# Moving units, scalings, a cast and two loads by a unit or two in a fused attention and GEGLU kernel

## The chip, the cores and the metric

The kernel runs on one core of a Trainium2 chip. The metric is device time in microseconds (us) of one execution. In the profiles' lines PE is TensorE (PEld its weight loads), DVE is VectorE, ACT is ScalarE, POOL is GpSimd and SPq is SyncE, which issues transfers. Profiles time the span, some 2.1 us shorter than the time of the run.

## The reference

```python
# q, k, v: (8, 8, 576, 64) f32; w_gate, w_val: (512, 1536); w_out: (1536, 512)
def phi(x): r = max(x, 0); return concat([r * cos_w, r * sin_w], -1)   # cos, sin of the position
kv  = einsum('bhsf,bhsd->bhfd', phi(k), v);  z = sum(phi(k), axis=2)
att = einsum('bhsf,bhfd->bhsd', phi(q), kv) / (einsum('bhsf,bhf->bhs', phi(q), z) + 1e-6)
x   = att, heads side by side: (4608, 512)
out = (gelu(x @ w_gate) * (x @ w_val)) @ w_out
```

## The kernel before

Tokens are cut into nine blocks: block 0 is batch 0 (576 tokens), blocks 1 to 8 are 512 tokens each, so that block 2 needs tiles 0 to 3 of batch 2's x. A *unit* is one gate matmul group and one value group for 128 of the 1536 columns. A *bank* is one of the eight parts of `ps`, the tile that TensorE writes its sums to; in this kernel it is written again only when another engine has read it. In block 0 a unit can be for a part of the tokens: (4,A) and (4,B) are column group 4 for tokens 0 to 255 and 256 to 575, (1,512) is group 1 for the last 64. The attention of the next batches is woven between the units. Engines run their instructions in the order written here (a manual schedule). From batch 1's keys on, all loads of q, k and v and all transposes by DMA are issued by SyncE, in this order too; the weights and batch 1's queries are loaded on GpSimd's queue, and a part of batch 0's keys on ScalarE's.

```python
def load(dst, t, b, ...):            # two DMAs, on SyncE if not said otherwise: odd and even tokens; q, k and v of one
    ...                              # batch are 1.18 MB each; qf, kf, vf are single buffers
def scale(f, j, which, eng, ...):    # relu(x * cos) or relu(x * sin) of one of 5 token tiles, f32 -> bf16
    ...                              # VectorE ("v") or ScalarE ("s"); sq: queries, sk: keys
def cast_v(b, h0, h1, eng="v"): ...  # v of heads h0 to h1 to bf16, beside a column of ones
def turn_q(b, j0, j1): nc.sync.dma_start_transpose(...)          # phi(q) transposed by DMA
def q_by_pe(b, j, bank, eng, ...): ...                           # the same by TensorE (batches 0, 1)
def kv_half(b, g, bank, eng="s"): ...                            # kv of 4 heads: 20 matmuls
def numer(b, t, bank, rows=128): numer_mm(...); numer_mm(...); xb = new_xb(); norm(xb, ...); return xb
def turn_x(b, t, xb): ...            # x tile transposed by DMA; xb has four buffers
def x_by_pe(b, t, xb, bank, eng, ...): ...   # the same by TensorE, then a copy by eng (batches 0, 1)

def gate(n, jt, c0, w, gb):          # 4 matmuls into bank gb, then gelu on ScalarE
def value(n, jt, c0, w, vb):         # 4 matmuls into bank vb, then hT = gel * ps on VectorE
def gv_unit(n, jt, c0, w, gb, vb): gate(...); value(...)

# block 0's end
    gv_unit(0, 0, 384, 128, 4, 6)
    X(4, 0, "v")()                   # x tile 4, by TensorE and VectorE
    gv_unit(0, 1, 384, 128, 5, 7)
    ...
# between blocks 0 and 1: output tiles of block 0, attention of batch 1
    x_by_pe(1, 0, y[0], 0, "s")
    o_part(0, 2, 4, 8, 12)
    sq(0, 1, "s"), sq(1, 1, "s")     # batch 2's queries, on ScalarE
    x_by_pe(1, 1, y[1], 1, "s")
    ...
    y4 = numer(1, 4, 0, 64)          # uses banks 0 and 1
    ...
    x_by_pe(1, 3, y[3], 7, "s")
    sq(0, 0, "v"), sq(1, 0, "v")
    o_part(0, 3, 5, 10, 12)
    x_by_pe(1, 4, y4, 6, "s")
    sq(2, 0, "v"), sq(2, 1, "s")
    turn_q(2, 0, 3)
    sq(3, 0, "v"), sq(3, 1, "s"), sq(4, 0, "v"), sq(4, 1, "s")
    turn_q(2, 3, 5)
    load_q(3)
# blocks 1 to 6: what follows unit u of block n, for batch b = n + 1
        s = 0 if n > 1 else -2
        put(2 + s, ...sk...); put(3 + s, ...sk...)
        put(4 + s, L(cast_v, b, 0, 4), L(cast_v, b, 4, 8, "s"))
        put(5 + (n == 1) + s, L(attn_step, b, 0))                # kv
        if b + 1 < B:
            if n > 1: put(3, L(load_q, b + 1))
            put(4 + s, L(load_k, b + 1)); put(5 + s, L(load_v, b + 1))
        for i in range(5):
            put(6 + (n == 1) + s + i, L(attn_step, b, i + 1))    # numer and turn_x of tile i
```

Of the kernel before, what the change touches and what calls it, by code (L numbers as in the profile page):

```python
# [16 lines left out]
def kernel(  # L17
# [111 lines left out]
    def scale(f, j, which, eng, h0=0, h1=H):  # L129
        dst, src = f  # L130
        col = (cos_c if which == 0 else sin_c)[:, j:j + 1]
        s, d = src[:, h0:h1, j, :], dst[:, j, h0:h1, which * D:(which + 1) * D]
        if eng == "v":
            nc.vector.tensor_scalar(d, s, col, 0.0, op0=ALU.mult, op1=ALU.max)  # L134
        else:
            nc.scalar.activation(d, s, AF.Relu, scale=col)  # L136

    def cast_v(b, h0, h1, eng="v"):
        cp = nc.vector.tensor_copy if eng == "v" else nc.scalar.copy
        cp(vx[b % 2][:, :, h0:h1, 0:D], vf[:, h0:h1].rearrange("p h j d -> p j h d"))  # L140
# [51 lines left out]
    def numer(b, t, bank, rows=128):  # L192

        numer_mm(b, t, bank, 0, rows)
        numer_mm(b, t, bank, 1, rows)
        xb = new_xb()
        norm(xb, bank, 0, 2, rows)
        return xb
# [14 lines left out]
    def gate(n, jt, c0, w, gb):  # L213

        p0 = starts[n] + c0
        for ct in range(CT):
            nc.tensor.matmul(  # L217
                ps[:, gb, 0:w], lhsT=wg_sb[:, ct, jt * 128:(jt + 1) * 128],
                rhs=xT[:, ct, p0:p0 + w], start=(ct == 0), stop=(ct == CT - 1),
            )  # L220
        gels[n, jt, c0] = gel = rot.tile([128, 512], FP32, name="gel", bufs=3)
        nc.scalar.activation(gel[:, 0:w], ps[:, gb, 0:w], AF.Gelu)  # L222

    def value(n, jt, c0, w, vb):

        p0 = starts[n] + c0
        for ct in range(CT):
            nc.tensor.matmul(  # L228
                ps[:, vb, 0:w], lhsT=wv_sb[:, ct, jt * 128:(jt + 1) * 128],
                rhs=xT[:, ct, p0:p0 + w], start=(ct == 0), stop=(ct == CT - 1),  # L230
            )
        gel = gels.pop((n, jt, c0))
        nc.vector.tensor_mul(hT[n % 2][:, jt, 64 + c0:64 + c0 + w], gel[:, 0:w], ps[:, vb, 0:w])  # L233

    def gv_unit(n, jt, c0, w, gb, vb, mid=()):
        gate(n, jt, c0, w, gb)
        for f in mid:
            f()
        value(n, jt, c0, w, vb)
# [15 lines left out]
    def o_part(n, m, bank, j0, j1):  # L255
        c0 = 128 * m - starts[n] + 64
        for jt in range(j0, j1):
            nc.tensor.matmul(  # L258
                ps[:, bank, :], lhsT=hT[n % 2][:, jt, c0:c0 + 128], rhs=wo_sb[:, jt, :],
                start=(jt == 0), stop=(jt == JT - 1),  # L260
            )
        if j1 == JT:
            o_store(m, bank)
# [49 lines left out]
    def load_v(b):  # L313
        load(vf, v, b)
# [20 lines left out]
    def x_by_pe(b, t, xb, bank, eng, c0=0, c1=CT):  # L335
        p0 = b * S + t * 128
        cp = nc.vector.tensor_copy if eng == "v" else nc.scalar.copy
        xb2 = xb.rearrange("p g h d -> p (g h d)")
        rows = 128 if t < NJ else 64
        view = ps[:, bank, 0:256].bitcast(BF16).rearrange("p (c t) -> p c t", c=CT)  # L340
        for ct in range(c0, c1):
            nc.tensor.transpose(  # L342
                out=view[:, ct, 0:rows], in_=xb2[0:rows, ct * 128:(ct + 1) * 128], identity=ident[0:rows, 0:rows],
            )
        cp(xT[:, c0:c1, p0:p0 + rows], view[:, c0:c1, 0:rows])  # L345

    def sq(j, which, eng, *h):
        scale(Q, j, which, eng, *h)
# [45 lines left out]
    A, Bw = (0, 256), (256, 320)  # L394
    xs = {1: x1}

    def X(t, bank, eng):
        return lambda: x_by_pe(0, t, xs[t], bank, eng)
# [29 lines left out]
    Y(4, 2)()  # L428
    gv_unit(0, 1, 256, 128, 5, 7)
    gv_unit(0, 0, 384, 128, 4, 6)  # L430
    X(4, 0, "v")()
    gv_unit(0, 1, 384, 128, 5, 7)
    gv_unit(0, 2, *Bw, 4, 6)
    gv_unit(0, 3, *Bw, 5, 7)
    gv_unit(0, 0, 512, 64, 0, 3)
# [11 lines left out]
    def L(f, *a):  # L447
        return lambda: f(*a)


    def T(t, bank, eng):
        q_by_pe(1, t, bank, eng)

    between = {
        (8, 0): (L(sq, 0, 0, "v"), L(sq, 0, 1, "s")),
        (8, 1): (L(sq, 1, 0, "v"), L(sq, 1, 1, "s")),
        (9, 0): (L(sq, 2, 0, "v"), L(sq, 2, 1, "s"), L(T, 0, 6, "v")),
        (9, 1): (L(sq, 3, 0, "v"), L(sq, 3, 1, "s"), L(T, 1, 7, "v")),
        (10, 0): (L(sq, 4, 0, "v"), L(sq, 4, 1, "s"), L(T, 2, 6, "v")),
        (10, 1): (L(load_q, 2), L(T, 3, 7, "v")),  # L460
        (11, 0): (L(T, 4, 6, "v"),),
        (11, 1): (L(carry, 0),),
    }
    for jt in range(4, 12):
        for i, (c0, w) in enumerate((A, Bw)):
            gv_unit(0, jt, c0, w, i, 3 - i)
            for f in between.get((jt, i), ()):
                f()
    for j in range(NJ + 1):
# [4 lines left out]
    sk(NJ, 1, "s")  # L474
    load_k(2)
    cast_v(1, 0, 4, "v")
    cast_v(1, 4, 8, "s")
    load_v(2)
    o_tile(0, 1, 5)
    kv_half(1, 0, 6, "s")  # L480
# [11 lines left out]
    norm(y[2], 6, 0, 2)  # L492
    x_by_pe(1, 0, y[0], 0, "s")
    o_part(0, 2, 4, 8, 12)
    sq(0, 1, "s"), sq(1, 1, "s")
    x_by_pe(1, 1, y[1], 1, "s")
    for g in (0, 1):
        numer_mm(1, 3, 2, g)
# [3 lines left out]
    y4 = numer(1, 4, 0, 64)  # L502
    o_part(0, 3, 5, 5, 10)
    x_by_pe(1, 3, y[3], 7, "s")
    sq(0, 0, "v"), sq(1, 0, "v")
    o_part(0, 3, 5, 10, 12)
    x_by_pe(1, 4, y4, 6, "s")
    sq(2, 0, "v"), sq(2, 1, "s")
    turn_q(2, 0, 3)
    sq(3, 0, "v"), sq(3, 1, "s"), sq(4, 0, "v"), sq(4, 1, "s")  # L510
# [13 lines left out]
    for n in range(1, 7):  # L524
        b = n + 1
        a = after[n]

        def put(u, *fs):
            a[u].extend(fs)

        if n > 1:
            put(0, L(sq, 0, 0, "v"), L(sq, 1, 0, "v"), L(sq, 1, 1, "v"), L(sq, 0, 1, "s"))
            put(1, L(sq, 2, 0, "v"), L(sq, 2, 1, "s"), L(turn_q, b, 0, 3))
            put(1, L(sq, 3, 0, "v"), L(sq, 4, 0, "v"), L(sq, 4, 1, "v"), L(sq, 3, 1, "s"), L(turn_q, b, 3, 5))
        s = 0 if n > 1 else -2
        put(2 + s, L(sk, 0, 0, "v"), L(sk, 1, 0, "v"), L(sk, 0, 1, "s"), L(sk, 1, 1, "s"))
        put(3 + s, L(sk, 2, 0, "v"), L(sk, 3, 0, "v"), L(sk, 4, 0, "v"))
        put(3 + s, L(sk, 2, 1, "s"), L(sk, 3, 1, "s"), L(sk, 4, 1, "s"))
        put(4 + s, L(cast_v, b, 0, 4), L(cast_v, b, 4, 8, "s"))
        put(5 + (n == 1) + s, L(attn_step, b, 0))  # L540
        if b + 1 < B:
            if n > 1:
                put(3, L(load_q, b + 1))
            put(4 + s, L(load_k, b + 1))
            put(5 + s, L(load_v, b + 1))
        for i in range(5):
            put(6 + (n == 1) + s + i, L(attn_step, b, i + 1))

# [49 lines left out]
```

## Time and profile before

| | us |
|---|---|
| time, median of 4 runs | 330.74 (330.67 to 330.81) |
| span of the profile | 328.99 |
| all 2,247 matmuls at their usual pitch | 314.18 |
| holes between matmuls | 8.73, of which 4.78 in the first 20 us |
| before the first matmul, after the last | 1.74, 4.18 |

The page's first lines: span, then busy time, share and number of instructions of each engine.

```profile
span 329.0 us, 5914 instructions
...
PE 320.1 (97%) x2247; PEld 168.3 (51%) x2247; DVE 172.4 (52%) x381; ACT 152.3 (46%) x273; POOL 21.4 (7%) x41
...
q14 instruction: 10, 0.08, 0.1%
```

TensorE bounds the kernel, but its 97% can't be used: matmuls overlap and their ends are modelled. The Trainium skill ("Trainium Kernel Development and Optimization", "Performance Expectations") calls matmul busy time a bad metric for how close a kernel is to its roofline, because matmuls are pipelined, and this case agrees: the share is 97% before and after, with spans 1.42 us apart. So *holes* are counted here from start to start: the usual distance from one matmul to the next is 0.216 us for 512 columns, 0.109 for 256, 0.056 for 128, 0.031 for 65, and what goes beyond it is a hole. A group of 4 with 512 columns takes 0.86.

Timeline of TensorE before (start, length, engine, line, out<-in, shape, count, and in brackets the modelled idle time and who ended it):

```profile
58.71 0.31 PE L169 MATMUL ps<-kv,qT 128*64 128x65 bf16 x4
59.38 0.29 PE L169 MATMUL ps<-kv,qT 128*64 128x65 bf16 x4 [0.35 <-ACT xT L345]
...
67.79 1.03 PE L228 MATMUL ps<-xT,wv_sb 128*128 128x512 bf16 x4
68.85 1.02 PE L217 MATMUL ps<-xT,wg_sb 128*128 128x512 bf16 x4
...
84.41 1.03 PE L228 MATMUL ps<-xT,wv_sb 128*128 128x512 bf16 x4
85.79 1.02 PE L217 MATMUL ps<-xT,wg_sb 128*128 128x512 bf16 x4 [0.35 <-DMA xT<-xb]
...
100.46 1.03 PE L228 MATMUL ps<-xT,wv_sb 128*128 128x512 bf16 x4
101.48 1.37 PE L153 MATMUL ps<-vx,kp 128*128 128x65 bf16 x40
```

From 84.41 a value group needs 0.86, so block 2's first gate could have started at 85.27; it started at 85.79: a hole of 0.51, though the bracket says 0.35. In the same way the hole at 59.38 is 0.51, the one at 68.85 is 0.20 and the one at 101.48 is 0.15; the last comes back in blocks 2 to 6.

ScalarE at that time, before (`qp` lines are scalings of queries, `xT` lines copies of x tiles, `gel` lines gelus):

```profile
57.52 1.33 ACT L136 ACTIVATE qp<-qf,sin_c 128x512 bf16<-128x512 f32 x2
58.76 1.06 ACT L345 COPY xT<-ps 128x512 bf16<-128x512 bf16 x2
61.11 0.58 ACT L345 COPY xT<-ps 128x512 bf16<-128x512 bf16 x1 [1.30 <-PE ps L342]
...
62.33 1.96 ACT L136 ACTIVATE qp<-qf,sin_c 128x512 bf16<-128x512 f32 x3
64.18 0.60 ACT L222 ACTIVATE gel<-ps 128x512 f32<-128x512 f32 x1
```

The two scalings at 57.52 hold up the copies behind them, and those free the bank that the matmuls at 59.38 wait for. From 61.11 to 70 no other line of ScalarE has idle time in front of it.

SyncE's issues around batch 2's x, before, and the end of the chain of waits there:

```profile
69.00 1.84 SPq L79 DMA_DIRECT2D qf<-in_q_dram  x2
70.95 1.32 SPq L79 DMA_DIRECT2D kf<-in_k_dram  x2
72.38 1.91 SPq L79 DMA_DIRECT2D vf<-in_v_dram  x2
75.53 8.22 SPq L204 DMA_TRANSPOSE xT<-xb  x4
```

```profile
82.53 3.12 DMA xT<-xb
...
85.79 1.02 PE ps L217 x4
```

The trace's landings: batch 3's k at 79.87, v at 83.75, and then all four transposes, issued over 8 us, within 1.5 us: 84.21, 84.71, 85.16, 85.65.

### The profile page before, as it was taken

What the parts mean: (1) busy time and instruction counts of PE and PEld (TensorE: products, weight loads), DVE (VectorE), ACT (ScalarE), POOL (GpSimd) and SP (SyncE); (2) the same over time, 40 slices, a digit from 0 to 9 for tenths busy, and PEclk for the clock granted to TensorE, in tenths of its full rate; (3) what the DMA queues carried; (4) which work ended last, traced back from release to release, by engine and by line L of the source; (5) the groups of instructions that cost most, each with busy time, mean ns of one, the idle gap of its engine ahead of it and who ended that gap; (6) DMA issues with size and microseconds to landing.
All of it is one profiled execution on the core that took longest, in us unless ns stands there. A gap on an engine that the chain in (4) does not pass through costs nothing.

```text
span 329.0 us, 5914 instructions
## 1 busy us (share of the span) xinstructions
PE 320.1 (97%) x2247; PEld 168.3 (51%) x2247; DVE 172.4 (52%) x381; ACT 152.3 (46%) x273; POOL 21.4 (7%) x41
## 2 busy tenths in 40 slices
PE   7799999999999999999999999999999999999994
PEld 3487876455445444544454445444544444444443
DVE  5895685668654657454835484557545322222210
ACT  6574665872564246523752376227622233222321
POOL 2650010000100010000100010001000100100000
PEclk9999999999999999999999999999999999999999
DMA  7999998799398936996599549974825121000024
GB/s 225 283 205 275 200 364 268 218 223 347 69 170 281 287 65 129 268 286 119 106 272 295 126 88 230 354 115 81 160 48 82 28 52 34 32 32 34 32 65 96
DMA packets 84635, 54.64 MB, mean 166 GB/s; under 512 B 49408, under 2 KB 79872, under 8 KB 84608
## 3 DMA queue, kind: packets, MB, share of 16 engines
q1 hardware_dynamic: 78096, 47.92, 58.8%
q0 software_dynamic: 6080, 5.90, 10.0%
q10 hardware_dynamic: 432, 0.46, 0.4%
q8 instruction: 17, 0.28, 0.3%
q14 instruction: 10, 0.08, 0.1%
HBM read 37.75 MB, written 9.44 MB: 143 GB/s over the span
## 4 chain that ended last, share of the span: by engine, by line
PE 92%; DMA 3%; DVE 2%; ACT 1%; issue 1%; POOL 0%; SPq 0%; DVEq 0%; POOLq 0%; ACTq 0%
PE ps L217 28%; PE ps L228 28%; PE ps L258 27%; PE ps L153 3%; PE ps L169 3%; DMA qf<-in_q_dram 2%; PE ps L323 1%; DMA xT<-xb 1%; PE ps L276 1%; PE ps L342 1%; ACT qp L136 0%; DVE vx L140 0%; DVE xb L184 0%; SPq L79 0%; DVE hT L233 0%
## 5 line engine op out<-in xcount | busy, mean ns | idle before, releaser
L233 DVE TENSOR_TENSOR hT<-gel,ps 128x512 bf16<-128x512 f32 (+5 forms) x126 | 76.3, 610 | 129.4 <-PE ps L228 125.8
L217 PE MATMUL ps<-xT,wg_sb 128*128 128x512 bf16 (+5 forms) x504 | 113.7, 348 | 0.8 <-DMA xT<-xb 0.3
L228 PE MATMUL ps<-xT,wv_sb 128*128 128x512 bf16 (+5 forms) x504 | 113.6, 349 | 0.0
L222 ACT ACTIVATE gel<-ps 128x512 f32<-128x512 f32 (+5 forms) x126 | 67.4, 537 | 78.0 <-PE ps L217 76.7
L258 PE MATMUL ps<-wo_sb,hT 128*128 128x512 bf16 x420 | 96.5, 379 | 0.0
L228 PEld LDWEIGHTS <-wv_sb 128*128 128x128 bf16 x504 | 47.8, 98 | 46.0
L217 PEld LDWEIGHTS <-wg_sb 128*128 128x128 bf16 x504 | 45.6, 98 | 41.1 <-issue 1.6
L258 PEld LDWEIGHTS <-hT 128*128 128x128 bf16 x420 | 40.0, 98 | 45.4
L287 ACT COPY o_sb<-ps 128x512 f32<-128x512 f32 x35 | 20.5, 585 | 74.6 <-PE ps L258 74.6
L184 DVE TENSOR_TENSOR xb<-ps,rec 128x512 bf16<-128x512 f32 (+2 forms) x41 | 27.8, 678 | 2.9 <-DMA xT<-xb 1.5
L136 ACT ACTIVATE kp<-kf,sin_c 128x512 bf16<-128x512 f32 (+1 forms) x41 | 25.4, 682 | 0.8 <-DMA kf<-in_k_dram 0.8
L134 DVE TENSOR_SCALAR qp<-qf,cos_c 128x512 bf16<-128x512 f32 x40 | 19.9, 540 | 0.0
L136 ACT ACTIVATE qp<-qf,sin_c 128x512 bf16<-128x512 f32 x29 | 19.8, 714 | 0.0
L169 PEld LDWEIGHTS <-qT 128*128 128x128 bf16 (+1 forms) x320 | 15.0, 98 | 9.1 <-issue 2.1
L134 DVE TENSOR_SCALAR kp<-kf,cos_c 128x512 bf16<-128x512 f32 (+1 forms) x45 | 18.7, 464 | 1.4 <-DMA kf<-in_k_dram 1.4
L169 PE MATMUL ps<-kv,qT 128*128 128x65 bf16 (+1 forms) x320 | 16.7, 193 | 0.5 <-ACT xT L345 0.4
L208 POOL COPY xT<-xr 128x256 bf16<-128x256 bf16 x6 | 2.7, 443 | 201.8 <-DMA xr<-xb 169.2
L153 PEld LDWEIGHTS <-kp 128*128 128x128 bf16 x320 | 10.8, 97 | 3.3 <-issue 2.0
L126 PE MATMUL ps<-junk 128*128 128x512 bf16 x35 | 10.0, 428 | 1.7 <-DVE par_i L103 1.7
L153 PE MATMUL ps<-vx,kp 128*128 128x65 bf16 x320 | 11.1, 193 | 0.1
L140 ACT CAST vx<-vf 128x1280 bf16<-128x1280 f32 (+1 forms) x9 | 10.2, 1136 | 1.2 <-DMA vf<-in_v_dram 1.2
L244 POOL COPY hT<-hT 128x768 bf16<-128x768 bf16 x8 | 7.6, 945 | 37.9 <-DVE hT L233 37.9
(56 smaller groups left out, 93.2 us busy)
## 6 DMA issues: line engine op xcount, KB each, us to landing
out_dram<-o_sb SPq DMA_DIRECT2D x38, 128.0 KB, 2.4
kf<-in_k_dram SPq DMA_DIRECT2D x7, 640.0 KB, 6.9
out_dram<-o_sb SPq DMA_DIRECT2D x16, 256.0 KB, 2.8
qf<-in_q_dram SPq DMA_DIRECT2D x6, 640.0 KB, 6.0
vf<-in_v_dram SPq DMA_DIRECT2D x6, 640.0 KB, 9.6
kf<-in_k_dram SPq DMA_DIRECT2D x7, 512.0 KB, 5.9
qf<-in_q_dram SPq DMA_DIRECT2D x6, 512.0 KB, 5.0
vf<-in_v_dram SPq DMA_DIRECT2D x6, 512.0 KB, 8.5
```

Source lines behind the costliest of these rows:

```text
L134: nc.vector.tensor_scalar(d, s, col, 0.0, op0=ALU.mult, op1=ALU.max)
L136: nc.scalar.activation(d, s, AF.Relu, scale=col)
L140: cp(vx[b % 2][:, :, h0:h1, 0:D], vf[:, h0:h1].rearrange("p h j d -> p j h d"))
L153: nc.tensor.matmul(ps[:, bank, (h % 4) * (D + 1):(h % 4 + 1) * (D + 1)], lhsT=kp[:, j, h, :], rhs=vx[b % 2][:, j, h, 0:D + 1], start=(j == ...
L169: nc.tensor.matmul(ps[0:rows, bank + g, (h % 4) * (D + 1):(h % 4 + 1) * (D + 1)], lhsT=qT[b % 2][:, t, h, 0:rows], rhs=kv[b % 2][:, h, 0:D ...
L184: nc.vector.tensor_tensor(xb[0:rows, g0:g1], nd[:, :, :, 0:D], rec[0:rows, 0:n, :, None].to_broadcast([rows, n, 4, D]), op=ALU.mult,)
L217: nc.tensor.matmul(ps[:, gb, 0:w], lhsT=wg_sb[:, ct, jt * 128:(jt + 1) * 128], rhs=xT[:, ct, p0:p0 + w], start=(ct == 0), stop=(ct == CT - 1),
L222: nc.scalar.activation(gel[:, 0:w], ps[:, gb, 0:w], AF.Gelu)
L228: nc.tensor.matmul(ps[:, vb, 0:w], lhsT=wv_sb[:, ct, jt * 128:(jt + 1) * 128], rhs=xT[:, ct, p0:p0 + w], start=(ct == 0), stop=(ct == CT - 1),
L233: nc.vector.tensor_mul(hT[n % 2][:, jt, 64 + c0:64 + c0 + w], gel[:, 0:w], ps[:, vb, 0:w])
L258: nc.tensor.matmul(ps[:, bank, :], lhsT=hT[n % 2][:, jt, c0:c0 + 128], rhs=wo_sb[:, jt, :], start=(jt == 0), stop=(jt == JT - 1),)
L287: nc.scalar.copy(o_sb, ps[:, bank, :])
```

## The change

It means to fill TensorE's holes: a unit in front of the transposes that wait for x tile 4; batch 1's queries scaled two units sooner; ScalarE's copies no longer behind two scalings; VectorE's half of v's cast a unit ahead of its use; and batch 3's k and v out of the way of batch 2's x. The diff, with the repeated lines of the query schedule cut:

```diff
     gv_unit(0, 0, 384, 128, 4, 6)
+    gv_unit(0, 1, 384, 128, 5, 7)
     X(4, 0, "v")()
-    gv_unit(0, 1, 384, 128, 5, 7)
+    gv_unit(0, 4, *A, 3, 1)             # (and left out of its old place)
 ...
-        (8, 0): (L(sq, 0, 0, "v"), L(sq, 0, 1, "s")),
+        (7, 0): (L(sq, 0, 0, "v"), L(sq, 0, 1, "s"), ),
 ...                                     # the other scalings and T() two units sooner alike
-    cast_v(1, 4, 8, "s")
+    cast_v(1, 4, 6, "v")
+    cast_v(1, 6, 8, "s")
 ...
-    sq(0, 1, "s"), sq(1, 1, "s")
     x_by_pe(1, 1, y[1], 1, "s")
 ...
     x_by_pe(1, 3, y[3], 7, "s")
+    sq(0, 1, "s"), sq(1, 1, "s")
     sq(0, 0, "v"), sq(1, 0, "v")
     o_part(0, 3, 5, 10, 12)
-    x_by_pe(1, 4, y4, 6, "s")
+    x_by_pe(1, 4, y4, 6, "v")
 ...
-        put(3 + s, L(sk, 2, 1, "s"), L(sk, 3, 1, "s"), L(sk, 4, 1, "s"))
-        put(4 + s, L(cast_v, b, 0, 4), L(cast_v, b, 4, 8, "s"))
+        put(3 + s, L(sk, 2, 1, "s"), L(sk, 3, 1, "s"), L(sk, 4, 1, "s"), L(cast_v, b, 0, 4))
+        put(4 + s, L(cast_v, b, 4, 8, "s"))
 ...
-            put(4 + s, L(load_k, b + 1))
-            put(5 + s, L(load_v, b + 1))
+            put(4 if n > 1 else 6, L(load_k, b + 1))
+            put(5 if n > 1 else 11, L(load_v, b + 1))
```

More of the change, by code (lines that the diff above doesn't have):

```diff
@@ L454 @@
     between = {
-        (8, 0): (L(sq, 0, 0, "v"), L(sq, 0, 1, "s")),
-        (8, 1): (L(sq, 1, 0, "v"), L(sq, 1, 1, "s")),
-        (9, 0): (L(sq, 2, 0, "v"), L(sq, 2, 1, "s"), L(T, 0, 6, "v")),
-        (9, 1): (L(sq, 3, 0, "v"), L(sq, 3, 1, "s"), L(T, 1, 7, "v")),
-        (10, 0): (L(sq, 4, 0, "v"), L(sq, 4, 1, "s"), L(T, 2, 6, "v")),
-        (10, 1): (L(load_q, 2), L(T, 3, 7, "v")),
-        (11, 0): (L(T, 4, 6, "v"),),
-        (11, 1): (L(carry, 0),),
+        (7, 0): (L(sq, 0, 0, "v"), L(sq, 0, 1, "s"), ),
+        (7, 1): (L(sq, 1, 0, "v"), L(sq, 1, 1, "s"), ),
+        (8, 0): (L(sq, 2, 0, "v"), L(sq, 2, 1, "s"), L(T, 0, 6, "v"), ),
+        (8, 1): (L(sq, 3, 0, "v"), L(sq, 3, 1, "s"), L(T, 1, 7, "v"), ),
+        (9, 0): (L(sq, 4, 0, "v"), L(sq, 4, 1, "s"), L(T, 2, 6, "v"), ),
+        (9, 1): (L(T, 3, 7, "v"), ),
+        (10, 0): (L(T, 4, 6, "v"), ),
+        (10, 1): (L(load_q, 2), ),
+        (11, 1): (L(carry, 0), ),
     }
@@ L465 @@
         for i, (c0, w) in enumerate((A, Bw)):
-            gv_unit(0, jt, c0, w, i, 3 - i)
+            if (jt, i) != (4, 0):
+                gv_unit(0, jt, c0, w, i, 3 - i)
             for f in between.get((jt, i), ()):
```

## The prediction

> **What bounds it.** TensorE. The page has it busy 320.1 of 329.0 us, but ends are modelled, so I take start-to-start times from its timeline: a 512-column matmul takes 0.216 us, 320 columns 0.136, 256 0.109, 128 0.056. All 2,247 matmuls at such rates make 314.2 us. The rest is 4.2 us of start and end and 8.7 us of holes. Of the holes 4.8 lie in the first 20 us, which the change leaves alone; of the other 4 only part can be won. TensorE's work stays (only order moves), its granted clock is 1.00: no 2% (6.6 us) either way.
>
> **Holes that the change touches (timeline, chain of waits):**
>
> 1. 25.37 us, 0.43: transposes of x's tile 4 wait for VectorE's xb (ends 25.31). One unit goes before them, but its value needs bank 7, which VectorE frees only at about 25.47, behind the same xb: about 0.15 is won. Unit (4,A) needs value weights that landed at 25.43, at about 26.3: no stall, thin slack. Then unit (4,B) follows (1,512) in bank 1 and waits for the later of two gelus (29.0, not 28.77): the hole at 28.82 grows from 0.13 to about 0.35. Sum: about +0.1.
>
> 2. Batch 1's q two units sooner: landed 34.14, scaled from about 35.7. TensorE has no hole in 39 to 52 us, and the keys' scaling still queues behind the block's last product. Worth 0.
>
> 3. 59.38, 0.51: numer(1,4) waits for ScalarE's copy of x tile 1, behind two scalings of 0.62 each. They move behind tile 3's copy: -0.51.
>
> 4. But ScalarE had been idle there, and from 61.1 to 70.9 it is busy without a gap and already makes TensorE wait 0.20 at 68.85. The two (1.25) go in there, a copy (0.27) leaves, TensorE comes 0.5 sooner. Gelu 0 ends at about 65.15 where gate 2 wants its bank at 64.7; gate 4 starts at about 69.3 for 68.85 before. So point 3 is given back, and more: 3 and 4 together +0.45.
>
> 5. 85.79, 0.51: block 2's first gate waits for the DMA transpose of batch 2's x. Four transposes issued from 75.53 to 82.53 all landed 84.21 to 85.65, just behind batch 3's v (83.75). The Trainium skill, "DMA: Bandwidth & Descriptors", "Queues, rings and completion order", says that each DMA engine consumes descriptors in ring order; these landings agree. With k(3) behind the first transpose and v(3) after the last, the last should land at about 85, needed at 85.8: -0.5. Thin: an unhindered one took 2.4 to 3.1.
>
> 6. Blocks 2 to 6: kv's first matmul waits 0.154 each for VectorE's cast of v (100.47 to 101.43 in block 2). VectorE is idle 97.4 to 99.9; the cast moves there: -0.154 x 5 = -0.77. ScalarE's half ends at 100.6, in time.
>
> Sum: +0.1 + 0.45 - 0.5 - 0.77 = -0.7 us.
>
> **Predicted 330.0 us, 8 in 10 between 329.2 and 331.0.** Faster by over 2%: 0.01; within: 0.98; slower: 0.01.
>
> **What would show it.** No hole before kv in blocks 2 to 6; none for DMA at about 85; none at 59; a new one of about 0.5 at gate 2 or 3 of block 1 (64 to 66) and more than 0.20 at gate 4, with ScalarE gapless; about 0.35 at 29 to 30.
>
> **What would make it wrong.** Slack in ScalarE's backlog that I don't see (then 329.3 or less); value weights later than 26.3 (up to a us lost); the transpose of x tile 3 still behind k(3), so that 0.5 stays; v(3) landing into the next queries' transposes.

## The result, and the profile after

332.13 us, median of 4 runs (331.28 to 332.55), against 330.74: ratio 1.0039, 95% interval 1.0017 to 1.0060. A ratio is the mean time of one kernel's fast runs over that of the other's of the same rounds, so not quite the ratio of the medians quoted. Within 2%, as forecast, but slower, and outside the range of 329.2 to 331.0. The profiled execution was the slowest of the four, 332.55, so the profile shows a little more than the typical difference.

```profile
span 330.4 us, 5918 instructions
...
PE 320.4 (97%) x2247; PEld 168.6 (51%) x2247; DVE 172.9 (52%) x383; ACT 151.7 (46%) x272; POOL 21.2 (6%) x41
...
q14 instruction: 11, 0.09, 0.1%
```

TensorE after, at the same places:

```profile
58.97 0.44 PE L169 MATMUL ps<-kv,qT 128*64 128x65 bf16 x8
...
64.08 1.03 PE L228 MATMUL ps<-xT,wv_sb 128*128 128x512 bf16 x4
65.52 1.02 PE L217 MATMUL ps<-xT,wg_sb 128*128 128x512 bf16 x4 [0.42 <-ACT gel L222]
...
68.11 1.03 PE L228 MATMUL ps<-xT,wv_sb 128*128 128x512 bf16 x4
69.54 1.02 PE L217 MATMUL ps<-xT,wg_sb 128*128 128x512 bf16 x4 [0.41 <-ACT gel L222]
70.59 1.02 PE L228 MATMUL ps<-xT,wv_sb 128*128 128x512 bf16 x4
...
85.29 1.03 PE L228 MATMUL ps<-xT,wv_sb 128*128 128x512 bf16 x4
87.46 1.02 PE L217 MATMUL ps<-xT,wg_sb 128*128 128x512 bf16 x4 [1.14 <-DMA xT<-xb]
...
102.13 1.03 PE L228 MATMUL ps<-xT,wv_sb 128*128 128x512 bf16 x4
102.99 1.37 PE L153 MATMUL ps<-vx,kp 128*128 128x65 bf16 x40
```

The hole at 59 is gone (one line of 8 where there were two of 4), and so is that before kv (102.13 + 0.86 = 102.99). New are 0.58 at gate 2 of block 1 (65.52), 0.57 at gate 4 (69.54) and 0.19 at the value after it (70.59); and block 2's first gate waits 1.30.

ScalarE after: the two scalings now stand at 61.34, and the first gelu comes at 64.89.

```profile
57.77 0.59 ACT L345 COPY xT<-ps 128x512 bf16<-128x512 bf16 x1
...
60.85 0.59 ACT L345 COPY xT<-ps 128x512 bf16<-128x512 bf16 x1 [1.20 <-PE ps L342]
61.34 1.33 ACT L136 ACTIVATE qp<-qf,sin_c 128x512 bf16<-128x512 f32 x2
...
63.04 1.95 ACT L136 ACTIVATE qp<-qf,sin_c 128x512 bf16<-128x512 f32 x3
64.89 0.58 ACT L222 ACTIVATE gel<-ps 128x512 f32<-128x512 f32 x1
```

Gate 0's matmuls (61.49 + 1.02) had ended at 62.51; its gelu stood behind five scalings. (Before, they had ended at 62.77 and the gelu came at 64.18, behind three of them: of the wait described here 1.0 us is new.) The Trainium skill ("TensorE: Matmul & The Clock Gate", "Architectural detail") says that ScalarE and VectorE are strict first in, first out, and that is what this shows: 2.4 us of waiting in line.

SyncE after, and the end of the chain there:

```profile
69.80 1.79 SPq L79 DMA_DIRECT2D qf<-in_q_dram  x2
76.41 1.20 SPq L204 DMA_TRANSPOSE xT<-xb  x1
77.72 2.29 SPq L79 DMA_DIRECT2D kf<-in_k_dram  x2
80.10 4.43 SPq L204 DMA_TRANSPOSE xT<-xb  x3
```

```profile
83.04 4.28 DMA xT<-xb
...
87.46 0.59 PE ps L217 x2
```

Landings after: the first transpose 80.35, k 83.58 and 85.81, the three other transposes 86.37, 86.85, 87.32. As before, they come just behind the load in front of them; but that load, now the keys, lands 2 us later than the values did.

Where the 1.42 us between the two profiles' spans are, by stretches of the span (no hole crosses their borders), and after the last matmul:

| stretch, us | holes before | holes after | difference | what |
|---|---|---|---|---|
| 0 to 20 | 4.78 | 4.71 | -0.07 | the start, not touched |
| 20 to 40 | 1.04 | 1.35 | +0.31 | the moved unit |
| 40 to 60 | 0.87 | 0.36 | -0.51 | the hole at 59 |
| 60 to 80 | 0.60 | 1.66 | +1.06 | gates 2 and 4, the value after it |
| 80 to 100 | 0.50 | 1.36 | +0.86 | block 2's first gate |
| 100 to the last matmul | 0.97 | 0.18 | -0.79 | kv in blocks 2 to 6 |
| after the last matmul's end | 4.18 | 4.69 | +0.51 | not foreseen |

The rows add up to +1.37; the remaining 0.05 lies in distances too small to be counted as holes.

### The profile page after: what moved, and what is told of

It is laid out like the page before. It is cut to its first block, busy times and chain, and to the rows that moved or that the text cites. A ratio compares the mean times of both kernels' runs of the same rounds, so it can differ in the third digit from the quotient of the medians.

```text
span 330.4 us, 5918 instructions
## 1 busy us (share of the span) xinstructions
PE 320.4 (97%) x2247; PEld 168.6 (51%) x2247; DVE 172.9 (52%) x383; ACT 151.7 (46%) x272; POOL 21.2 (6%) x41
## 4 chain that ended last, share of the span: by engine, by line
PE 90%; DMA 3%; ACT 2%; SPq 1%; DVE 1%; issue 1%; POOL 0%; DVEq 0%; POOLq 0%
PE ps L258 27%; PE ps L217 27%; PE ps L228 27%; PE ps L169 3%; PE ps L153 3%; DMA vf<-in_v_dram 2%; DMA xT<-xb 1%; PE ps L323 1%; SPq L79 1%; PE ps L276 1%; PE ps L342 1%; ACT qp L136 1%; ACT kp L136 1%; ACT gel L222 1%; DVE xb L184 0%
## 5 line engine op out<-in xcount | busy, mean ns | idle before, releaser
L126 PE MATMUL ps<-junk 128*128 128x512 bf16 x35 | 10.7, 453 | 1.7 <-DVE par_i L103 1.7
```

Of the source, the lines that this page charges most:

```text
L126: nc.tensor.matmul(ps[:, bank, :], lhsT=junk[:, 0:128], rhs=junk, start=True, stop=True)
```

## The experiments

Twelve runs, in three jobs of four, two of them the kernel before and the changed kernel once more; the four of a job share a chip and the runs of the kernel before. All gave correct results. "Holes" are read from each one's profile.

| kernel | median us (lowest to highest) | ratio to before (95%) |
|---|---|---|
| p4_cast | 330.18 (329.99 to 330.46) | 0.9986 (0.9973 to 0.9999) |
| p5_loads | 331.24 (330.43 to 331.65) | 1.0015 (1.0000 to 1.0029) |
| p3_scale | 331.28 (330.92 to 331.49) | 1.0017 (1.0004 to 1.0030) |
| p1_order | 330.89 (330.75 to 331.27) | 1.0006 (0.9992 to 1.0020) |
| after_again | 331.91 (331.41 to 332.38) | 1.0042 (1.0029 to 1.0055) |
| keys_last | 330.88 (330.67 to 331.19) | 1.0014 (1.0001 to 1.0027) |
| best0 | 329.63 (329.12 to 330.66) | 0.9977 (0.9961 to 0.9993) |
| best1 | 328.91 (328.36 to 329.26) | 0.9953 (0.9939 to 0.9967) |
| before_again | 330.79 (330.35 to 330.81) | 0.9992 (0.9975 to 1.0009) |
| no_split | 331.56 (330.69 to 332.22) | 1.0017 (0.9999 to 1.0035) |
| pad | 331.57 (331.19 to 334.35) | 1.0031 (1.0003 to 1.0060) |
| no_scale | 330.97 (330.55 to 331.58) | 1.0001 (0.9984 to 1.0018) |

The kernel before, run in all three jobs, had medians of 330.57, 330.50 and 330.77, and spread over about 1.3 us or more in each. A difference of 0.3 us is therefore read from holes, not from times.

### p4_cast: the cast alone

```diff
-        put(3 + s, ..., L(sk, 4, 1, "s"))
-        put(4 + s, L(cast_v, b, 0, 4), L(cast_v, b, 4, 8, "s"))
+        put(3 + s, ..., L(sk, 4, 1, "s"), L(cast_v, b, 0, 4))
+        put(4 + s, L(cast_v, b, 4, 8, "s"))
```

> The kernel before with one part alone: VectorE's half of the cast of v a unit sooner. Theory: the 0.154 us holes in front of kv's first matmul in blocks 2 to 6 go (-0.77), and in block 1 the cast now stands ahead of a product on VectorE that TensorE needs (0.1 to 0.2 back): -0.6 us, 330.1. Rival (the cast takes VectorE time that the next product needs in every block): no gain or a loss, new holes in front of value matmuls in blocks 2 to 6.

Measured: ratio 0.9986, that is 0.46 us faster. No hole before kv in blocks 2 to 6, and 0.19 at the value after gate 4 in block 1, as expected. Block 2's first gate had no hole either in this profile, although its loads weren't touched; "before_again" below comes back to that. Why the hole before kv goes, in two lines of VectorE each: before, the cast starts behind a product and ends just before kv; in the changed kernel (where it has the same place, some 1.5 us later in the span) it lies in VectorE's idle time.

```profile
100.47 0.95 DVE L140 CAST vx<-vf 128x1280 bf16<-128x1280 f32 x1
101.59 0.69 DVE L233 TENSOR_TENSOR hT<-gel,ps 128x512 bf16<-128x512 f32 x1 [0.17 <-PE ps L228]
```

```profile
99.02 0.95 DVE L140 CAST vx<-vf 128x1280 bf16<-128x1280 f32 x1
101.54 0.69 DVE L233 TENSOR_TENSOR hT<-gel,ps 128x512 bf16<-128x512 f32 x1 [1.57 <-PE ps L228]
```

### p5_loads: the later keys and values alone

```diff
-            put(4 + s, L(load_k, b + 1))
-            put(5 + s, L(load_v, b + 1))
+            put(4 if n > 1 else 6, L(load_k, b + 1))
+            put(5 if n > 1 else 11, L(load_v, b + 1))
```

> The kernel before with one part alone: batch 3's keys loaded between the first and second transpose of batch 2's x, its values after the last. Theory: now the transposes 2 to 4 stand behind the keys' load, which itself is issued some 6 us later than before; the hole at block 2's first gate grows from 0.51 to 1.2 or more: +0.7 us or more. Rival (the longer hole of the changed kernel came from the whole of block 1 running late, queries of batch 3 included, and not from the keys' place): the hole goes to nearly 0, -0.5 us.

Measured: ratio 1.0015, about 0.5 us slower with an interval that touches none, and a hole of 0.36. Both sides missed the hole: it neither went nor grew to 1.2. The order of landings is as the theory has it (k at 84.14, then the three transposes to 85.61), but the keys landed early enough to do no more harm than the values had done. This run alone didn't settle the question; keys_last does.

### p3_scale: the scalings and the copy alone

```diff
-    sq(0, 1, "s"), sq(1, 1, "s")
     x_by_pe(1, 1, y[1], 1, "s")
 ...
     x_by_pe(1, 3, y[3], 7, "s")
+    sq(0, 1, "s"), sq(1, 1, "s")
 ...
-    x_by_pe(1, 4, y4, 6, "s")
+    x_by_pe(1, 4, y4, 6, "v")
```

> The kernel before with one part alone: two scalings of batch 2's queries moved on ScalarE behind the copy of x tile 3, the copy of tile 4 to VectorE. Theory: the hole of 0.51 at 59.4 goes, but gate 2 of block 1 waits about 0.6 and gate 4 about 0.5 instead of 0.2, since ScalarE is busy without a gap there: +0.4 us, 331.2. Rival (the waits there come from the cast of v and not from the scalings): -0.5 us, 330.2, no new wait at gate 2.

Measured: ratio 1.0017, 0.56 us slower. The hole at 59 is gone; gate 2 waits 0.58 and gate 4 0.57, the same as with the whole change, and without any cast moved. The rival falls.

### p1_order: the rest alone

The first three parts of the diff: the unit of block 0, batch 1's queries, the split cast.

> The kernel before with the rest of the change alone: a unit moved in block 0, batch 1's queries two units sooner, its cast of v split. Theory: the hole at 25.4 stays about 0.4 in another place (value waits for its bank), the hole at 28.8 grows from 0.13 to 0.36: +0.2 us, all of it from the moved unit; the queries and the split give nothing. Rival (the earlier queries or the split do help): a gain, 330.5 or less.

Measured: ratio 1.0006; the interval holds 1, so the time decides nothing. The holes are as expected: 0.40 at the value that waits for its bank (25.69), 0.36 at gate (4,B) (30.10), and nothing different from 40 to 60 us, where the queries and the split act.

### after_again and keys_last: where batch 3's keys stand

after_again is the changed kernel. keys_last has one edit to it:

```diff
-            put(4 if n > 1 else 6, L(load_k, b + 1))
+            put(4 if n > 1 else 10, L(load_k, b + 1))
```

> The changed kernel unaltered, for a second profile and more times beside its variants. If the parts add up (measured alone: -0.46, +0.5, +0.56, +0.2) it is +0.8 us over the kernel before; if it is again +1.3, some of the parts make each other worse. Theory: the first gate of block 2 waits for the last transpose of batch 2's x by an amount that varies from run to run (0.4 to 1.3), while the waits of 0.58 and 0.57 at gates 2 and 4 of block 1 come back to within 0.02.

> The changed kernel, batch 3's keys loaded after the last transpose of batch 2's x (a unit before its values) and not between the first and the second. Theory: the transposes have no load in front of them, all land by 85 and the hole at block 2's first gate goes to 0.1 or less: 0.5 to 1.3 us below the changed kernel of this job; the keys land at about 91, in time for block 2. Rival (the transposes are late by themselves, from xb and the queue's issue): the hole stays above 0.4 and the time within 0.3 us of the changed kernel.

Measured: after_again 331.91, by its ratio +1.4 us and not the +0.8 of a plain sum, with holes of 0.58, 0.57 and 0.19 in block 1 and 1.02 at block 2's first gate (1.30 in the first profile). keys_last 330.88, 1.03 below, and block 2's first gate has no hole at all:

```profile
76.11 7.20 SPq L204 DMA_TRANSPOSE xT<-xb  x4
...
85.45 1.30 SPq L79 DMA_DIRECT2D kf<-in_k_dram  x2
```

```profile
84.99 1.03 PE L228 MATMUL ps<-xT,wv_sb 128*128 128x512 bf16 x4
85.85 1.03 PE L217 MATMUL ps<-xT,wg_sb 128*128 128x512 bf16 x4
```

The transposes landed at 80.31, 80.93, 82.61 and 84.57, the last 2.5 us after its issue, and block 2's first gate (85.85) started without waiting. The keys landed at 91.6 and the values at 95.0, with no hole at block 2's kv. So the hole belongs to the keys' place in the queue. The rival falls.

### best0 and best1: scalings forward instead of back

best0 is the kernel before with the cast moved in blocks 2 to 6 only, and:

```diff
     kv_half(1, 1, 7, "v")
+    sq(0, 1, "s"), sq(1, 1, "s")
 ...
     o_part(0, 2, 4, 8, 12)
-    sq(0, 1, "s"), sq(1, 1, "s")
```

best1 moves more of them, and the first query transpose:

```diff
     o_tile(0, 1, 5)
+    for j in range(3):
+        sq(j, 0, "v")
     kv_half(1, 0, 6, "s")
     kv_half(1, 1, 7, "v")
+    for j in range(4):
+        sq(j, 1, "s")
+    turn_q(2, 0, 3)
 ...                                     # and these left out further down
```

> A version meant to win: the kernel before, VectorE's half of the cast sooner in blocks 2 to 6 only, and the two sine scalings of batch 2's queries moved on ScalarE forward into its idle stretch at 53 to 56 us, and not back as the change does. Theory: the hole of 0.51 at 59.4 goes, ScalarE has 1.25 us less to do from 61 on so the 0.20 at gate 4 goes too, the five of 0.154 go: -1.4 us against the kernel before, less what the transposes take back at block 2's first gate (up to 0.5). Rival (the scalings in that stretch delay kv's or x's copy): holes at 53 to 57.

> As best0, but four sine and three cosine scalings of batch 2's queries go forward, and its first query transpose too, so that batch 3's queries, keys and values are loaded some microseconds sooner, ahead of batch 2's x transposes. Theory: as best0, and no hole at block 2's first gate either: -1.6 to -1.9 us. Rival (the earlier loads and the query transposes collide with batch 2's keys and values, which are on the queues till 60): new holes for kp or vx in block 1, and a gain under 1 us.

Measured: best0 329.63, ratio 0.9977, 0.8 us faster where 1.4 less up to 0.5 was expected. The holes at 59 and before kv are gone. Block 2's first gate waits only 0.02 in this profile, but its loads weren't touched, so this isn't shown to be the edit's doing (see "before_again"). The 0.20 at gate 4 stayed, and the expectation was wrong there by its own logic: in the kernel before the two scalings stood at 57.5, so moving them forward took nothing off ScalarE after 61. best1, which takes two more sine scalings out of that stretch, has no hole there. It is 328.91 us, ratio 0.9953: 1.6 us faster than the kernel before and 3.0 below the changed kernel of the same job. Batch 3's values landed at 81.42 and the last transpose at 83.32, needed at about 84.2 (the gate follows the first transpose's issue by 9.74 us, and that is at 74.45). Its list of TensorE's waits (engine, line, waited for: us, times, longest) ends with x tile 4 of block 0:

```profile
PE ps L126 <- DVE par_i L103: 1.7, 1, 1.7
PE ps L323 <- ACT qp L136: 0.5, 1, 0.5
PE ps L217 <- ACT xT L345: 0.3, 1, 0.3
PE ps L342 <- DVE xb L184: 0.3, 1, 0.3
```

### before_again, no_split, pad: the spread, and the long end

After the last matmul's end the changed kernel took 4.69 us (4.90 in after_again, 4.59 in keys_last) against 4.18 before; the four parts alone and best0, best1 took 4.14 to 4.16. The first three have 578 recorded VectorE instructions (sequencer's included; the page counts without), the others 574 or 576. In the DMA packets of the first three a transfer of 8192 bytes on the queue q14 lies among the last store's packets: in the changed kernel from 327.54 to 328.12, while the store was issued at 326.38, its last packet on its own queue ended at 328.60, and it landed at 329.14, 2.76 us after its issue. In the kernel before the same store took 2.24. In the others the transfer of q14 comes after the end.

no_split is the changed kernel without the split of the cast; pad is the kernel before with four spare instructions:

```diff
-    cast_v(1, 4, 6, "v")
-    cast_v(1, 6, 8, "s")
+    cast_v(1, 4, 8, "s")
```

```diff
             for f in after[n][jt]:
                 f()
+            if n == 7 and jt in (4, 5, 7, 8):
+                nc.vector.memset(spare, 0.0)      # [1, 8], read by nobody
```

> The kernel before, for a second profile. Theory: the hole at block 2's first gate is a race between TensorE and the last transpose and differs from profile to profile (0.51 in the first), while all the other holes are the same to 0.02; the time from the last matmul's end to the end of the span is 4.2 again. Rival (the hole is fixed, and the spread of 1.3 us of this kernel's times comes from elsewhere): 0.5 again.

> The changed kernel without the split of the cast of batch 1's v (ScalarE casts heads 4 to 7 alone), which takes two instructions off VectorE. From the changed kernel's last matmul to its end it took 4.7 and 4.9 us, against 4.15 to 4.2 in every kernel with 576 or fewer VectorE instructions; it has 578, and a transfer of 8192 bytes on the instruction queue falls among the last store's packets. Theory (VectorE's next block of instructions is fetched there): with 576 the end is 4.15 to 4.2 again, no such transfer before the end, and the kernel is 0.5 us faster than the changed one. Rival (the long end belongs to the change in another way, or to chance): 4.6 to 4.9 again, time unchanged.

> The kernel before with four spare memsets of 8 elements on VectorE in block 7, where it is mostly idle: 578 instructions instead of 574. Theory: the 8192 byte transfer appears among the last store's packets, the end takes 4.6 to 4.9 us instead of 4.2, the kernel is 0.5 us slower than before, and no hole on TensorE changes. Rival: no difference.

Measured, the queue's line of the page (packets, MB, share): no_split, then pad. The bytes tell, not the count: no_split's 11th packet is one of 64 bytes, pad's one of 8192.

```profile
q14 instruction: 11, 0.08, 0.1%
```

```profile
q14 instruction: 11, 0.09, 0.1%
```

no_split ends 4.17 us after its last matmul, and no 8192 byte transfer falls there: as expected. Its ratio of 1.0017, against 1.0039 and 1.0042 for the changed kernel in other jobs, fits 0.5 us, but its interval reaches to 1.0035, so the end in the profile is the evidence. pad ends 4.91 us after its last matmul, with a transfer of 8192 bytes at 326.29, and is slower than the kernel before, 1.0031 (1.0003 to 1.0060), though one run of 334.35 among its six carries a part of that. Its last store took 2.98 us to land, that of no_split 2.24. Both ways the end follows two or four VectorE instructions. That the transfer holds instructions for VectorE is inferred from this. One expectation of pad missed: its hole at block 2's first gate is 0.67, not that of the kernel before.

before_again: 0.35 at block 2's first gate, where the first profile had 0.51, and the other holes of block 1 and of kv within 0.01. With p4_cast (0), best0 (0.02), p1_order (0.24), p3_scale (0.31) and pad (0.67), which also leave that gate's loads alone, this hole lies anywhere from 0 to 0.67. The first 20 us differ too, against the expectation: 4.28 to 5.11 in the profiles with all matmuls recorded. Between the two profiles of the kernel before, these two places make up the difference in span (0.39 us); that they make the whole spread of its times isn't shown. (In the profiles of the first job 35 of the matmul records are missing; each leaves a false hole of 0.21 to 0.22, left out here.)

### no_scale: the changed kernel without the scalings' move

The edit is that of p3_scale, undone.

> The changed kernel without the move of the two scalings (and with tile 4's copy back on ScalarE), 576 VectorE instructions. Theory: the hole at 59.4 is back (0.51), gates 2 and 4 wait 0 and about 0.2, so 0.44 is won there, and 0.5 at the end: 0.9 to 1.0 us below the changed kernel. What the hole at block 2's first gate does tells whether its size (1.0 to 1.3 with all parts, 0.36 with the loads alone) needs the scalings: below 0.5 if it does, near 1 if not.

Measured: 330.97, ratio 1.0001, and 4.17 at the end. The hole at 59 is back (0.52), gate 2 waits 0 and gate 4 0.20, as expected. By the ratios of the other jobs (1.0039, 1.0042) it is some 1.3 us below the changed kernel, more than the 0.9 to 1.0 expected. At block 2's first gate 0.57: between 0.36 (the loads alone) and 0.97 to 1.30 (three profiles with all parts). So the parts don't simply add there.

## Why the prediction was wrong, point by point

Its sum was -0.7 us, and the profiles show +1.4. Term by term:

1. *The moved unit, "+0.1".* Measured +0.31, mis-sized. The hole before x tile 4 only changed hands: 0.40 at the value that waits for its bank, of 0.43. Of "about 0.15 is won" 0.03 came. The new 0.36 at gate (4,B) was right ("about 0.35").
2. *Batch 1's queries, 0.* Right: nothing changed from 40 to 59 us.
3. *and 4. The scalings, "+0.45".* Right: -0.51, then 0.58 at gate 2 and 0.37 more at gate 4, sum +0.44; p3_scale shows it alone.
5. *The loads, "-0.5".* **This is the step that failed**: "With k(3) behind the first transpose and v(3) after the last, the last should land at about 85, needed at 85.8". The last landed at 87.32 and was needed at 86.16. The prediction named the mechanism (the queue's order; the Trainium skill, "DMA: Bandwidth & Descriptors", "Queues, rings and completion order") and then didn't follow it through. Before the change the keys had been issued at 70.95 and had landed by 79.9; only the values were in the transposes' way. The change puts the keys, of the same size, in that place, and issues them at 77.72 to 80.01. keys_last shows that the place is what costs: the same kernel with the keys behind the transposes has no hole there. The 0.5 to be won was itself one profile's value of a hole that is 0 to 0.67 with the loads where they were. The risk was listed ("the transpose of x tile 3 still behind k(3), so that 0.5 stays"), but as the hole staying and not as growing to 1.0 to 1.3.
6. *kv, "-0.77".* Right: -0.79 from 100 us on. Not foreseen was +0.19 in block 1, where VectorE has no idle stretch and the earlier cast stands in front of a product; p4_cast shows it.
7. *Not in the sum at all:* the end of the kernel, +0.5 to +0.7, a block of 8192 bytes on the instruction queue q14 while the last store goes out. pad and no_split show that it follows VectorE's number of instructions.

With the measured terms, 0.31 + 0.44 + 0.19 + 0.79 (block 2's first gate, 1.30 - 0.51) - 0.79 + 0.51 = +1.45; with the first 20 us (-0.07) it is 1.38, of 1.42 seen.

Partly open: why block 2's first gate waits 0.36 with the loads alone and 1.0 to 1.3 with everything. In all these profiles the gate needs the transposes some 9.74 us after the first of them is issued, and the hole follows the landing of the last load in front of them. Counted from the first transpose's issue:

| what lands in front | where | lands after, us | hole, us |
|---|---|---|---|
| values | p4_cast, best0, p1_order | 7.61, 7.75, 7.98 | 0, 0.02, 0.24 |
| values | p3_scale, before_again, before, pad | 8.05, 8.09, 8.22, 8.40 | 0.31, 0.35, 0.51, 0.67 |
| keys | p5_loads, no_scale | 8.50, 8.68 | 0.36, 0.57 |
| keys | no_split, after_again, changed | 9.10, 9.13, 9.39 | 0.97, 1.02, 1.30 |

So what grows is the time until the keys have landed. The keys' issue on SyncE starts 1.31 us after the first transpose's in all five and takes 1.85 us with the loads alone, 2.14 in no_scale, 2.29 (changed) to 2.48 with all parts. That is about all of the growth over p5_loads in after_again and no_split, and half of it in the changed kernel's first profile. The traces show one thing in step with it: a transfer of 16384 bytes on the other instruction queue, q8, runs during the first transpose. It ends 2.20 us after that transpose's issue with the loads alone, 2.36 in no_scale and 2.51 to 2.70 with all parts, and the first of the two key DMAs is through its issue 0.27 to 0.40 us later each time. Whether that transfer holds the issue back wasn't tried.

## What to carry to other kernels

On a shared DMA queue a load that is moved later doesn't get out of the way: ask what stands right behind its new place, and put it behind the last transfer that something waits for, or well ahead. On an engine that works in order, move work from in front of a critical instruction to an idle stretch, forward if there is one (best1), and not into a stretch without gaps. Where a change is worth tenths of a microsecond, sum the holes of every stage, the end of the kernel included, and count each engine's instructions. And take more than one profile before counting on a hole that waits for a transfer: this one was 0 to 0.67 us with the same loads in the same place.

## What the Trainium skill lacked or had wrong

- "Runtime: NRT & Kernel Launch", "Instruction fetch mechanics": it says that engines refill instructions in 16 KiB blocks and that crossing a block is mostly hidden. Here 17 transfers of 16384 bytes came on one instruction queue, q8, but those of q14, which VectorE's count moves, are of 8192 bytes, and one that falls on the last store isn't hidden: 4.59 to 4.91 us from the last matmul's end to the end of the span, against 4.14 to 4.18 in the ten other profiles.
- "DMA: Bandwidth & Descriptors", "Issuing engines are not separate DMA queues": it calls the time on the sequencer to start a DMA usually small relative to the DMA itself. For transposes it wasn't: in the kernel before, the one issued at 85.02 took 1.19 us to issue of 2.43 from issue to landing, and one of the four before it 2.50 of 5.22. The two key loads took 1.3 us to issue before the change and 2.3 in the changed kernel, behind a transpose.
- "DMA: Bandwidth & Descriptors", "Queues, rings and completion order": ring order agrees (transposes landed within 1.5 us, behind the load in front of them), but no page says that a DMA transpose between on-chip buffers queues behind loads from HBM in this way, with what it costs: 3.1 to 8.7 us from issue to landing for the four before the change, 2.4 to 2.5 for the quickest nine of the same profile.
